# Zero stores of a key and value gradient: one region per group split over 15 and 4 transfer engines, and four regions moved to the end

## The chip, the core and the metric

The kernel runs on one core of a Trainium2 chip. A core has five engines that work on their own instruction queues: PE (TensorE: matrix products and transposes), DVE (VectorE), ACT (ScalarE), POOL (GpSimd) and SP (SyncE, which here only issues transfers). Data between the chip's memory (HBM) and the on-chip memory (SBUF) is moved by sixteen DMA engines, which here are called transfer engines. A transfer (DMA) is issued by SP, ACT or POOL, is cut into packets, and the packets are spread over the transfer engines. Results of matrix products land in PSUM, from which ACT or DVE must copy them ("evacuate" them) to SBUF.

The metric is device time in microseconds (us) of one execution; less is better.

## What is computed

The reference is one decoding step of a transformer block, and the gradient of all its inputs:

```python
xn = layernorm(x)
out = x + attention(xn, k_cache, v_cache, wq, wo) + geglu_ffn(xn, w_gate, w_up, w_down)
out, vjp = jax.vjp(...)
return (out, *vjp(grad_out))
```

Sizes: 4 sequences (b), one new token each, width 512; 32 query heads that share 8 heads (g) of keys and values (four query heads to a head), head width 128; a cache of 4096 positions, of which attention sees only the last 1024; a feed-forward layer of width 1792. All in bf16.

The outputs are the block's output, the gradient of x, and the gradients of the caches and the weights. The gradients of the two caches, dK and dV, have the full shape (4, 8, 4096, 128), although only positions 3072 to 4095 can be different from zero. So each of the 32 pairs (b, g) of dK and of dV has a region of 3072 x 128 bf16 = 768 KB of zeros that must be written. There are 64 such regions, 50.3 MB.

## The kernel before

The feed-forward layer with its gradients comes first. Then the attention part runs over four groups t = 0 to 3 of two key and value heads each (GP = 2), in the loop of lines 766 to 787. For a group:

- masks(t) makes the masked copies of the queries and of the output's gradient (POOL).
- scores(t, 0) transposes the group's keys on TensorE, evacuates the transposed tiles with DVE and multiplies them with the queries; scores(t, 1), also called the dP step, does the same with the values and the output's gradient. The step k = 1 runs the softmax of this group in hooks between its parts (softmax(t), where E_f and P_b are made on ACT and P_x on POOL).
- softmax_d(t) makes the gradient through the softmax. Pieces d1 and d2 put the dV and dK products on a list.
- pre(t + 1) makes queries and the output's gradient of the next group, odq(t) and fin(t) close this one, load_next(t) issues loads for a later group, and dw(t) puts the pieces of the weight products (wo and wq) on the list.

The list is bg. Its pieces are small: one product on TensorE, one evacuation to a staging tile and, with the last piece of a tile, a store. tick(n) (L323) takes up to n of them; it is called between the steps of scores and elsewhere, so that pieces of one group run while the scores of the next are made. Staging tiles are stg_dv and stg_dk (dvdk, around L540; 1 MB per store, 1024 positions of one head for four sequences), osb_o and osb_q (dw, L559 and L571; 512 KB per store). Those stores are issued by SP (helper store, L105), each at its place in SP's order.

The zeros are written by zeros(n) (L303 to L318). It takes the next n regions of dV's and dK's lists, up to four in one transfer, from a zeroed tile ztile in SBUF: 64 of its rows (every second partition) of 12,288 bytes write one region, so that each of the sixteen transfer engines has four rows. These stores are issued by ACT. A manual dependency orders each behind the latest evacuation on ACT, so it takes its place in ACT's order there and waits for nothing of it. The table ZN says how many regions go out in scores(t, k) for head g, after the second of the four tiles:

```python
ZN = ((0, 4, 4, 4), (0, 4, 4, 2), (2, 4, 4, 4), (4, 4, 4, 4))   # index: t, then 2k + g
...
                if q == 1:
                    zeros(ZN[t][GP * k + g])
```

Further regions go out in the feed-forward part, after scores(0, 0), after softmax_d in the last group (zeros(4)), and what remains goes out after the loop (zeros(2 * B * G), where nothing is left here). SP's and ACT's transfers are two hardware queues (q1 and q10 on the page), POOL's a third (q0); q8 brings instructions.

After the loop and the last pieces, the sums over groups are transposed (f_ps), and DVE makes the block's output and the gradient of x, two small stores of four rows (out_b, dx_b).

Of the kernel before, what the change touches and what calls it, by code (L numbers as in the profile page):

```python
# [14 lines left out]
P = 128  # L15
# [3 lines left out]
def kernel(  # L19
# [27 lines left out]
    nc = tc.nc  # L47
# [7 lines left out]
    K0 = Sk - W  # L55
# [5 lines left out]
    GP = 2  # L61
# [26 lines left out]
    last = []  # L88
    chain = []

    def evac(out, in_, n, half=False, eng=None):

        eng = "dve" if half else eng or ("act" if chain else None)
        ca, cd = (190 + n) / 1.2, (120 + (n / 2 if half else n)) / 0.96
        if eng is None:
            eng = "act" if load["act"] + ca <= load["dve"] + cd else "dve"
        load[eng] += ca if eng == "act" else cd
        if eng == "act":
            last.append(nc.scalar.copy(out=out, in_=in_))  # L99
            return last[-1]  # L100
        return nc.vector.tensor_copy(out=out, in_=in_)  # L101

    def store(eng, out, in_, kind, apart):

        d = eng.dma_start(out=out, in_=in_)  # L105
        for k in apart:
            tc.declare_no_dep(d.ins, group=k, reason="stores write disjoint parts of the outputs")
        tc.add_to_no_dep_group(kind, d.ins)
        return d
# [81 lines left out]
    ZP = P // 2  # L191
    ZW = K0 // ZP * Dh
    ztile = const.tile([P, ZW], BF16, name="ztile")
# [83 lines left out]
    def load_w(t):  # L277
        eng = nc.gpsimd if t else nc.sync
        pool = wpool[t % 2]
        wo_t[t] = pool.tile([P, HG, D], BF16, name="wo_sb", tag="wo")  # L280
        eng.dma_start(out=wo_t[t][:], in_=wo_v[t])
        wq_t[t] = pool.tile([P, ND, CW], BF16, name="wq_sb", tag="wq")
        eng.dma_start(out=wq_t[t][:], in_=wq_v[t])

    def load_kv(t, k, g):
        d_, src, nm = ((k_t, A_k_cache, "kb"), (v_t, A_v_cache, "vb"))[k]
        tl = kvpool[(GP * t + g) % (2 * GP)].tile([P, J, Dh], BF16, name=nm, tag=nm)
        (nc.gpsimd if GP * t + g > GP else nc.sync).dma_start(out=tl[:].rearrange("p j d -> p (j d)"),
                          in_=src[:, t * GP + g, K0:Sk, :].rearrange("b (m j) d -> m b (j d)", j=J))
        d_[(t, g)] = tl  # L290
# [9 lines left out]

    zruns = deque([og, 0] for og in (out_2, out_3))

    def zeros(n):  # L303


        zs = ztile[0:P:P // ZP, :]
        while n > 0 and zruns:
            og, r = zruns[0]
            w = min(n, B * G - r, GP * 2)
            zsrc = bass.AP(tensor=zs.tensor, offset=zs.offset, ap=[list(zs.ap[0]), [0, w], [1, ZW]])  # L310
            zdst = og.rearrange("b g s d -> (b g) s d")[r:r + w, 0:K0, :].rearrange("r (m j) d -> m r (j d)", m=ZP)
            z = store(nc.scalar, zdst, zsrc, "zeros", ["rest", "zeros"])
            tc.add_manual_dep(z.ins, last[-1].ins.name,
                              mybir.DependencyInfo(mybir.DependencyClass.NoSync, mybir.DependencyReason.DATA))
            n -= w
            zruns[0][1] += w
            if zruns[0][1] == B * G:
                zruns.popleft()  # L318
# [4 lines left out]
    def tick(n):  # L323
        for _ in range(min(n, len(bg))):
            bg.popleft()()
# [62 lines left out]
                                        in1=msk[:, :, g].unsqueeze(2).broadcast_to([P, NQ, Dh]), op=ALU.mult)  # L388
            st[t][nm] = mr

    ZN = ((0, 4, 4, 4), (0, 4, 4, 2), (2, 4, 4, 4), (4, 4, 4, 4))

    def scores(t, k, hooks):

        lf = (qm, dom)[k]
        blks = (k_t, v_t)[k]
        ps = ps_a.tile([P, WQ], FP32, name="S_ps", tag=("S", "dP")[k])
        for g in range(GP):
            for q in range(NQ):
                T_ps = ps_w.tile([P, JQ, P], BF16, name="T_ps", tag="w")  # L400
                for jj in range(JQ):
                    nc.tensor.transpose(T_ps[:, jj, :], blks[(t, g)][:, q * JQ + jj, :], ident[:])  # L402
                T_sb = tsb.tile([P, WQ, B], BF16, name="T_sb", tag="T", bufs=4)
                evac(T_sb[:].rearrange("p n b -> p (n b)"), T_ps[:].rearrange("p j m -> p (j m)"), 1024, half=True)
                s = q * GP + g
                for b in range(B):
                    nc.tensor.matmul(ps[b * RG:(b + 1) * RG, :], lhsT=lf[:, b, s * RG:(s + 1) * RG],  # L407
                                     rhs=T_sb[:, :, b], start=(g == 0 and q == 0),
                                     stop=(g == GP - 1 and q == NQ - 1), tile_position=(0, b * RG))
                for f in hooks.get(g * NQ + q, ()):  # L410
                    f()
                tick(2 if k or q % 2 else 1)
                if q == 1:
                    zeros(ZN[t][GP * k + g])
        st[t][("S", "dP")[k]] = ps[:]

    def by_batch(src, nm, eng):
# [308 lines left out]
    for f4 in range(NF4):  # L726
        held = {}
        n = min(4, NF - 4 * f4)
# [30 lines left out]
    with tc.tile_pool(name="stage", bufs=4, reuse_waits="tile") as stage, \  # L759
            tc.tile_pool(name="wodd", bufs=1, reuse_waits="tile") as wodd:  # L760
        wpool.append(wodd)
        kvpool.append(wodd)
        load_w(1)
        for k in range(2):
            load_kv(1, k, 1)
        for t in range(NT):
            if t == 0:
                pre(t, {})
            masks(t)
            scores(t, 0, {})  # L770
            zeros(2 if t == 0 else 0)
            scores(t, 1, softmax(t))
            d1, d2 = softmax_d(t)
            zeros(4 if t == NT - 1 else 0)
            if t + 1 < NT:
                pre(t + 1, {0: [d1], 2: [d2]})
            else:
                tick(2)
                d1()
                tick(6)  # L780
                d2()
                tick(2)
            odq(t)
            fin(t)
            load_next(t)
            tick(len(bg))
            dw(t)
        tick(len(bg))
        zeros(2 * B * G)


        acc_r = kvp.tile([P, 2, ND, B, RB], FP32, name="acc_r", tag="kb")
        nc.vector.tensor_copy(out=acc_r[:], in_=acc[:].unsqueeze(4).broadcast_to([P, 2, ND, B, RB]))
        fin_ps = []
        for o in range(2):
            f_ps = ps_w.tile([P, ND, P], FP32, name="f_ps", tag="w")
            for c in range(ND):
                nc.tensor.transpose(f_ps[:, c, :], acc_r[:, o, c].rearrange("p b r -> p (b r)"), ident_f[:])
            fin_ps.append(f_ps[:])
        acc_o, acc_d = fin_ps[0].rearrange("p c d -> p (c d)"), fin_ps[1].rearrange("p c d -> p d c")  # L800

        def adj(x):
            return x[:].rearrange("p (d c) -> p d c", c=ND)

        out_b = kvp.tile([P, D], BF16, name="out_b", tag="vb")
        nc.vector.tensor_tensor(out=out_b[:], in0=acc_o, in1=x_b[:], op=ALU.add)
        nc.sync.dma_start(out=out_0.rearrange("b s d -> (b s) d"), in_=out_b[0:P:RB, :])

        s1 = const.tile([P, 1], FP32, name="s1")
        nc.vector.reduce_sum(out=s1[:], in_=acc_d, axis=AX.XY)  # L810
        pr = kvp.tile([P, D], FP32, name="pr", tag="vb")
        s2 = const.tile([P, 1], FP32, name="s2")
        nc.vector.tensor_tensor_reduce(out=adj(pr), in0=acc_d, in1=adj(xn_f), scale=1.0, scalar=0.0,
                                       op0=ALU.mult, op1=ALU.add, accum_out=s2[:])
        nm1 = const.tile([P, 1], FP32, name="nm1")
        nc.vector.tensor_scalar(out=nm1[:], in0=s1[:], scalar1=-1.0 / D, scalar2=None, op0=ALU.mult)
        nm2 = const.tile([P, 1], FP32, name="nm2")
        nc.vector.tensor_scalar(out=nm2[:], in0=s2[:], scalar1=-1.0 / D, scalar2=None, op0=ALU.mult)
        nc.vector.scalar_tensor_tensor(out=adj(pr), in0=adj(xn_f), scalar=nm2[:, 0:1], in1=acc_d,
                                       op0=ALU.mult, op1=ALU.add)  # L820
        nc.vector.tensor_scalar(out=pr[:], in0=pr[:], scalar1=nm1[:, 0:1], scalar2=rstd[:, 0:1],
                                op0=ALU.add, op1=ALU.mult)
        dx_b = kvp.tile([P, D], BF16, name="dx_b", tag="kb")
        nc.vector.tensor_tensor(out=dx_b[:], in0=pr[:], in1=dy_b[:], op=ALU.add)
        nc.sync.dma_start(out=out_1.rearrange("b s d -> (b s) d"), in_=dx_b[0:P:RB, :])
# [30 lines left out]
```

## Time and profile before

| | us |
|---|---|
| median of 4 runs | 281.8 (281.27 to 282.4) |
| profiled execution, its own time | 281.17 |
| its span in the profile | 279.4 |
| PE busy | 210.5 (75%) |
| DVE busy | 158.4 (57%) |
| ACT busy | 114.8 (41%) |
| POOL busy | 56.0 (20%) |
| time of ACT's transfers (q10: 50.34 MB, 4400 packets) | 42.7% of 16 engines' span |
| time of SP's transfers (q1: 44.58 MB, 12304 packets) | 39.3% |
| time of POOL's transfers (q0: 16.78 MB, 2688 packets) | 15.0% |

All times of the trace count from the start of the span; the profiled execution's own time has 1.8 us more than the span. A row of slices on the page divides the span into 40 equal parts of 7 us, and a digit is the busy share in tenths; the row DMA is the mean over the sixteen transfer engines. ACT issues the zero stores in 0.61 us each: 14 of 3072 KB (from issue to landing 22.3 us in the median) and four of 1536 KB (12.7 us). A transfer lands when the last of its packets has.

The last zero stores are issued at 206.84, 214.12, 220.85, 232.52 and 237.50 us, the first four of them from scores of t = 3, the last behind softmax_d. The last evacuation of a dK piece by ACT ends at 254.8, the first osb_o evacuation of the last weight products on ACT begins at 254.94, and the last osb_q store is issued at 265.95.

### The profile page before, as it was taken

What the parts mean: (1) busy time and instruction counts of PE and PEld (TensorE: products, weight loads), DVE (VectorE), ACT (ScalarE), POOL (GpSimd) and SP (SyncE); (2) the same over time, 40 slices, a digit from 0 to 9 for tenths busy, and PEclk for the clock granted to TensorE, in tenths of its full rate; (3) what the DMA queues carried; (4) which work ended last, traced back from release to release, by engine and by line L of the source; (5) the groups of instructions that cost most, each with busy time, mean ns of one, the idle gap of its engine ahead of it and who ended that gap; (6) DMA issues with size and microseconds to landing.
All of it is one profiled execution on the core that took longest, in us unless ns stands there. A gap on an engine that the chain in (4) does not pass through costs nothing.

```text
span 279.4 us, 7185 instructions
## 1 busy us (share of the span) xinstructions
PE 210.5 (75%) x3126; PEld 137.2 (49%) x3132; DVE 158.4 (57%) x336; ACT 114.8 (41%) x214; POOL 56.0 (20%) x56
## 2 busy tenths in 40 slices
PE   1968976988669879968597978699897765889300
PEld 0856854755445565535365645356664442455200
DVE  6955644555357647654685355477754636276620
ACT  1321642454335236636334445373453442535300
POOL 3890003140200345020006600200520020020000
PEclk9985997799797998999999799999999999597955
DMA  7999999999999999999999999999999999999970
GB/s 239 448 389 429 421 403 396 414 415 425 422 425 426 423 418 417 411 435 421 431 414 354 409 425 426 425 423 427 423 415 427 422 429 422 427 429 425 422 283 20
DMA packets 19423, 112.15 MB, mean 401 GB/s; under 512 B 1456, under 2 KB 5056, under 8 KB 10432
## 3 DMA queue, kind: packets, MB, share of 16 engines
q10 hardware_dynamic: 4400, 50.34, 42.7%
q1 hardware_dynamic: 12304, 44.58, 39.3%
q0 software_dynamic: 2688, 16.78, 15.0%
q8 instruction: 24, 0.39, 0.5%
q14 instruction: 7, 0.06, 0.0%
HBM read 30.68 MB, written 81.01 MB: 400 GB/s over the span
## 4 chain that ended last, share of the span: by engine, by line
PE 45%; DMA 27%; DVE 18%; issue 3%; POOL 1%; ACT 1%; ACTq 0%; DVEq 0%; SPq 0%
DMA out_dram<-osb_q 13%; DMA out_dram<-stg_dk 9%; PE T_ps L402 7%; PE kv_ps L540 6%; DMA out_dram<-osb_g 5%; PE S_ps L407 5%; DVE T_sb L101 4%; PE woT_ps L339 3%; PE wgT_ps L745 3%; DVE woT L101 2%; PE od_ps L512 2%; PE acc_ps L213 2%; PE wqT_ps L598 2%; PE dwg_ps L718 2%; PE dwo_ps L559 2%
## 5 line engine op out<-in xcount | busy, mean ns | idle before, releaser
L101 DVE COPY T_sb<-T_ps 128x1024 bf16<-128x1024 bf16 x64 | 43.8, 690 | 41.0 <-PE T_ps L402 40.5
L99 ACT CAST stg_dv<-kv_ps 128x512 bf16<-128x512 f32 x57 | 30.0, 595 | 31.3 <-PE kv_ps L540 27.9
L99 ACT CAST stg_dk<-kv_ps 128x512 bf16<-128x512 f32 x40 | 22.2, 592 | 37.3 <-PE kv_ps L540 23.8
L540 PE MATMUL kv_ps<-domr,P_x 128*128 128x512 bf16 x63 | 21.5, 404 | 9.6 <-POOL P_x L420 4.8
L387 POOL TENSOR_TENSOR domr<-r,msk 128x512 bf16<-128x512 bf16 x8 | 8.2, 1040 | 73.0 <-DVE r L380 73.0
L402 PE MATMUL T_ps<-ident,kb 128*128 128x128 bf16 x256 | 22.7, 228 | 0.0
L402 PEld LDWEIGHTS <-kb 128*128 128x128 bf16 x256 | 17.8, 103 | 8.6 <-issue 5.8
L99 ACT CAST osb_g<-dwg_ps 128x512 bf16<-128x512 f32 (+1 forms) x28 | 14.1, 539 | 19.0 <-PE dwg_ps L718 8.2
L540 PE MATMUL kv_ps<-qmr,dS_x 128*128 128x512 bf16 x60 | 20.8, 430 | 0.5 <-DVE stg_dk L101 0.2
L402 PE MATMUL T_ps<-ident,vb 128*128 128x128 bf16 x256 | 20.8, 223 | 0.1
L99 ACT CAST osb_o<-dwo_ps 128x512 bf16<-128x512 f32 x25 | 14.6, 586 | 14.0 <-PE dwo_ps L559 13.3
L402 PEld LDWEIGHTS <-vb 128*128 128x128 bf16 x256 | 16.1, 100 | 6.9 <-issue 5.0
L420 POOL TENSOR_TENSOR P_x<-P_b,bmsk 128x1024 bf16<-128x1024 bf16 x4 | 7.6, 1893 | 57.3 <-ACT P_b L468 57.3
L407 PE MATMUL S_ps<-T_sb,dom 128*32 128x256 bf16 x128 | 12.7, 387 | 8.3 <-DVE T_sb L101 7.8
L99 ACT CAST osb_q<-dwq_ps 128x512 bf16<-128x512 f32 x25 | 14.1, 589 | 10.6 <-PE dwq_ps L571 6.1
L101 DVE CAST stg_dk<-kv_ps 128x512 bf16<-128x512 f32 x24 | 16.0, 682 | 1.9 <-PE kv_ps L540 1.8
L101 DVE COPY woT<-woT_ps 128x1024 bf16<-128x1024 bf16 x16 | 11.0, 688 | 9.1 <-PE woT_ps L339 9.1
L407 PE MATMUL S_ps<-T_sb,qm 128*32 128x256 bf16 x128 | 13.1, 387 | 4.0 <-DVE T_sb L101 4.0
L101 DVE COPY wqT<-wqT_ps 128x1024 bf16<-128x1024 bf16 x16 | 11.0, 686 | 5.3 <-PE wqT_ps L598 5.2
L101 DVE COPY wgT<-wgT_ps 128x1024 bf16<-128x1024 bf16 x14 | 9.7, 691 | 7.5 <-PE wgT_ps L745 7.5
L407 PEld LDWEIGHTS <-dom 128*32 128x32 bf16 x128 | 5.3, 93 | 17.1 <-issue 15.3
L559 PE MATMUL dwo_ps<-dyz,od_x 128*128 128x512 bf16 x32 | 13.5, 461 | 0.0
(214 smaller groups left out, 399.6 us busy)
## 6 DMA issues: line engine op xcount, KB each, us to landing
out_dram<-ztile ACTq DMA_DIRECT2D x14, 3072.0 KB, 22.3
out_dram<-stg_dv SPq DMA_DIRECT2D x8, 1024.0 KB, 24.8
out_dram<-stg_dk SPq DMA_DIRECT2D x8, 1024.0 KB, 17.7
out_dram<-ztile ACTq DMA_DIRECT2D x4, 1536.0 KB, 12.7
kb<-in_A_k_cache_dram POOLq DMA_DIRECT2D x5, 1024.0 KB, 20.6
vb<-in_A_v_cache_dram POOLq DMA_DIRECT2D x5, 1024.0 KB, 25.9
out_dram<-osb_o SPq DMA_DIRECT2D x8, 512.0 KB, 15.8
out_dram<-osb_q SPq DMA_DIRECT2D x8, 512.0 KB, 28.4
```

The costliest lines, as they stand in the source:

```text
L99: last.append(nc.scalar.copy(out=out, in_=in_))
L101: return nc.vector.tensor_copy(out=out, in_=in_)
L213: nc.tensor.matmul(ps[:, c, :], lhsT=lf(c), rhs=rhs, start=(k == 0), stop=(k == len(terms) - 1))
L339: nc.tensor.transpose(wT_ps[:, i, c, :], wo_sb[:, 2 * h2 + i, c * P:(c + 1) * P], ident[:])
L387: nc.gpsimd.tensor_tensor(out=mr[:, g], in0=st[t]["r4"][:, k, :].unsqueeze(1).broadcast_to([P, NQ, Dh]), in1=msk[:, :, g].unsqueeze(2).bro ...
L402: nc.tensor.transpose(T_ps[:, jj, :], blks[(t, g)][:, q * JQ + jj, :], ident[:])
L407: nc.tensor.matmul(ps[b * RG:(b + 1) * RG, :], lhsT=lf[:, b, s * RG:(s + 1) * RG], rhs=T_sb[:, :, b], start=(g == 0 and q == 0), stop=(g = ...
L420: eng.tensor_tensor(out=dst[:].rearrange("p j (m b) -> p (j m) b", b=B), in0=src[:].unsqueeze(2).broadcast_to([P, WQ, B]), in1=bmsk[:].uns ...
L512: nc.tensor.matmul(od_ps[r0:r0 + rep * B, 0, :], lhsT=pT[:, j % JQ, (j // JQ) * GP + g:P:NS], rhs=blks[(t, g)][:, j, :], start=(j == 0), s ...
L540: nc.tensor.matmul(mps[:].rearrange("p q d -> p (q d)"), lhsT=src[:, jj, :], rhs=mr[:, g].rearrange("p q d -> p (q d)"), start=True, stop= ...
L559: nc.tensor.matmul(mps[:], lhsT=X[:].rearrange("p h d -> p (h d)")[:, g * rep + i:CW:HG], rhs=dyz[:], start=True, stop=True)
L745: nc.tensor.transpose(wT_ps[:, i, c, :], wsb[:, c, fc * P:(fc + 1) * P], ident[:])
```

## The change

In each group, the call of zeros in scores(t, 0) for the second head is made with part=True. Where this takes a full set of four regions, it issues three transfers in place of one: three regions as before (2304 KB), then of the fourth region the first 60 rows (720 KB, four rows on each of fifteen engines), then the last 4 rows (48 KB, one row on each of four engines). ACT thus issues 26 transfers in place of 18, with the same bytes.

The last entry of ZN for t = 3 goes from 4 to 0, so that no zeros go out in the dP step of the last group for its second head. In place of it, after dw(3) has put the last weight products on the list, two pieces are taken, four regions are issued, and then the rest of the list runs. In ACT's order the zeros(4) behind softmax_d stays where it was among the pieces, and now writes the four regions that the removed call wrote; the new call stands behind the first evacuation of osb_o.

The order of instructions on PE, DVE, POOL and SP is the same as before.

```diff
--- before.py
+++ after.py
@@ -300,18 +300,24 @@
 
     zruns = deque([og, 0] for og in (out_2, out_3))
 
-    def zeros(n):
-
-
-        zs = ztile[0:P:P // ZP, :]
+    def zeros(n, part=False):
+
+
         while n > 0 and zruns:
             og, r = zruns[0]
             w = min(n, B * G - r, GP * 2)
-            zsrc = bass.AP(tensor=zs.tensor, offset=zs.offset, ap=[list(zs.ap[0]), [0, w], [1, ZW]])
-            zdst = og.rearrange("b g s d -> (b g) s d")[r:r + w, 0:K0, :].rearrange("r (m j) d -> m r (j d)", m=ZP)
-            z = store(nc.scalar, zdst, zsrc, "zeros", ["rest", "zeros"])
-            tc.add_manual_dep(z.ins, last[-1].ins.name,
-                              mybir.DependencyInfo(mybir.DependencyClass.NoSync, mybir.DependencyReason.DATA))
+            cuts = [(0, w, 0, ZP)] if not part or w < n else [(0, w - 1, 0, ZP), (w - 1, 1, 0, ZP - ZP // 16),
+                                                              (w - 1, 1, ZP - ZP // 16, ZP)]
+            for r1, nr, m0, m1 in cuts:
+                if nr == 0:
+                    continue
+                zs = ztile[(P // ZP) * m0:(P // ZP) * m1:P // ZP, :]
+                zsrc = bass.AP(tensor=zs.tensor, offset=zs.offset, ap=[list(zs.ap[0]), [0, nr], [1, ZW]])
+                zdst = og.rearrange("b g s d -> (b g) s d")[r + r1:r + r1 + nr, 0:K0, :].rearrange(
+                    "r (m j) d -> m r (j d)", m=ZP)[m0:m1]
+                z = store(nc.scalar, zdst, zsrc, "zeros", ["rest", "zeros"])
+                tc.add_manual_dep(z.ins, last[-1].ins.name,
+                                  mybir.DependencyInfo(mybir.DependencyClass.NoSync, mybir.DependencyReason.DATA))
             n -= w
             zruns[0][1] += w
             if zruns[0][1] == B * G:
@@ -388,7 +394,7 @@
                                         in1=msk[:, :, g].unsqueeze(2).broadcast_to([P, NQ, Dh]), op=ALU.mult)
             st[t][nm] = mr
 
-    ZN = ((0, 4, 4, 4), (0, 4, 4, 2), (2, 4, 4, 4), (4, 4, 4, 4))
+    ZN = ((0, 4, 4, 4), (0, 4, 4, 2), (2, 4, 4, 4), (4, 4, 4, 0))
 
     def scores(t, k, hooks):
 
@@ -411,7 +417,7 @@
                     f()
                 tick(2 if k or q % 2 else 1)
                 if q == 1:
-                    zeros(ZN[t][GP * k + g])
+                    zeros(ZN[t][GP * k + g], part=(k, g) == (0, 1))
         st[t][("S", "dP")[k]] = ps[:]
 
     def by_batch(src, nm, eng):
@@ -785,6 +791,8 @@
             load_next(t)
             tick(len(bg))
             dw(t)
+        tick(2)
+        zeros(4)
         tick(len(bg))
         zeros(2 * B * G)
 
```

## Prediction

> **What bounds the kernel now.** I read the page's row of DMA shares first, then the last windows of the timeline, then the chain that ended last, then the two issuing queues between 199 and 240 us. The page:
>
> ```profile
> DMA  7999999999999999999999999999999999999970
> GB/s 239 448 389 429 421 403 396 414 415 425 422 425 426 423 418 417 411 435 421 431 414 354 409 425 426 425 423 427 423 415 427 422 429 422 427 429 425 422 283 20
> ...
> HBM read 30.68 MB, written 81.01 MB: 400 GB/s over the span
> PE 45%; DMA 27%; DVE 18%; issue 3%; POOL 1%; ACT 1%; ACTq 0%; DVEq 0%; SPq 0%
> ```
>
> The transfer engines are full in 38 of 40 slices, at some 425 GB/s. TensorE is busy 75% of the span, so bytes are the first limit, and only the last two slices are not full. The windows there (columns: span, length, busy time of PE, PEld, DVE, ACT, POOL, granted clock, DMA share, GB/s):
>
> ```profile
> 258.00:268.00 10.00, 3.09 (x16) 1.61 (x14) 6.65 (x13) 2.93 (x6) 0.00 (x0) 0.82 1.00 419
> 268.00:270.00 2.00, 0.00 (x0) 0.00 (x0) 0.00 (x0) 0.00 (x0) 0.00 (x0) 0.50 0.75 297
> 270.00:272.00 2.00, 0.00 (x0) 0.00 (x0) 0.00 (x0) 0.00 (x0) 0.00 (x0) 0.50 0.40 157
> 272.00:278.00 6.00, 0.00 (x0) 0.00 (x0) 0.00 (x0) 0.00 (x0) 0.00 (x0) 0.50 0.07 26
> 278.00:279.40 1.40, 0.00 (x0) 0.00 (x0) 0.00 (x0) 0.00 (x0) 0.00 (x0) 0.50 0.00 0
> ```
>
> From 272 to 278 us nothing computes, and the share is 0.07, which is one sixteenth: a single transfer engine is still at work. Chained by size, queue and end, the packet records give the same: the sixteen engines run without a gap from 2 us, fifteen end between 268.6 and 272.4, one at 277.9. The mean is 270.95, so this engine is 7 us behind the mean and 5.5 behind the next. Its packets are a little slower, not more. A store is landed when its last engine is done, so the lag also shows in landings: the osb_q store issued at 225.65 has fifteen sixteenths at 249.96 and the last at 261.48.
>
> The chain passes through such landings:
>
> ```profile
> 199.59 25.99 DMA out_dram<-stg_dk
> ...
> 225.65 35.83 DMA out_dram<-osb_q
> ...
> 261.58 0.59 ACT osb_q L99
> ```
>
> Why a store waits for a landing is read in the queues (ACT's timeline; the release in brackets):
>
> ```profile
> 214.12 0.61 ACTq L105 DMA_DIRECT2D out_dram<-ztile  x1
> ...
> 220.85 0.61 ACTq L105 DMA_DIRECT2D out_dram<-ztile  x1
> ...
> 223.18 0.51 ACT L468 ACTIVATE P_b<-E_f,rr 128x256 bf16<-128x256 f32 x1 [1.48 <-DVE rr L466]
> ...
> 237.50 0.61 ACTq L105 DMA_DIRECT2D out_dram<-ztile  x1
> 238.15 3.03 ACT L99 CAST stg_dv<-kv_ps 128x512 bf16<-128x512 f32 x6 [3.41 <-DMA out_dram<-osb_o]
> ```
>
> The zero store at 237.50 starts 0.03 us after the osb_o store of 208.98 lands (237.47), a tile that has nothing to do with it. In the order of the program it is the eighth SP or ACT transfer after that one. The osb_q store of 225.65 follows the landing of the eighth before it (stg_dk, 225.58) in the same way, the zero store of 232.52 the stg_dk of 205.88 (232.50), the stg_dv store of 242.99 the osb_o of 214.51 (242.93). So a transfer of these two queues starts only when the eighth before it has landed, and one late engine holds both queues.
>
> **The change, part by part.**
>
> *The split.* Once in each of the four groups a store of four regions (3,072 KB, 64 rows of 12,288 B per region, four rows per engine) becomes one of three regions, one of 60 rows and one of 4 rows. Bytes and rows stay. A 12,288-byte packet took 457 ns from one to the next. The engine that has no part in the 60 rows loses 4 rows x 4 groups = 16 x 0.457 = 7.3 us; four others gain one row each per group, 4 x 0.457 = 1.8 us. The four that the existing four-row transfers (out_b, dx_b) use end at 269.7; with 1.8 they end at 271.5. If the late engine is the one left out, it ends at 277.9 - 7.3 = 270.6, and the last is the next in line, 272.4: 5.5 us gained. If it is another, its bytes are as before and it ends at 277.9 or later: 0. It can't gain rows if it isn't among the four, and it isn't: its chain has no packet of the four-row transfers.
>
> *Which engine that is.* No row names an engine. The late chain carries neither the four-row transfers nor any of the 24 packets of instruction loading (which go over eight engines, three each), which leaves four engines of sixteen. A transfer in less than sixteen parts always uses the same four, so parts are given out from one side, and the engine that fifteen parts leave out is at the other side. The chance lies between one in four (any of the four engines) and one; I take a half, a little nearer to the first end.
>
> [...]
>
> *Eight more issues on ACT.* Four times two, 0.61 us each (median 608 ns in the row of ztile) = 4.9 us of ACT's queue, 1.2 per group. ACT is busy 41%, and waits 27.9 us for kv_ps in stg_dv evacuations, so three of the four lie beside idle time; in the last group I count 0 to 1.2 and take 0, as that group's chain waits for transfers.
>
> *Eight more places in the round of eight.* This is the price. In the last group the three stores stand at 214.12, 214.7 and 215.3. The third now waits for the stg_dv store of 189.30 (landed 219.19): ACT stands 3.9 us, with the osb_q evacuations behind it, and TensorE behind these once its PSUM buffers are full. SP's osb_q of 217.38 now waits for the stg_dk of 199.59 (225.58), 8.2 us; behind it is only the next osb_q, which left at 225.65 anyway. ACT's store of 220.85 now waits for the stg_dk of 205.88 (232.50): up to 11.6 us, with P_b (223.18) behind it, for which POOL's P_x and the dv products wait. The store of 237.50 waits for the osb_o of 214.51 instead of 208.98: 5.5 us. Where landings stay, that is bounded by 0 (all hidden) and 3.9 + 11.6 - 3.4 (the wait that goes) = 12 us on the compute path; I take 7, as TensorE is idle 4.1 of the 19 us from 214 to 233 and 3.6 of the 5 after. Where the late engine is relieved, three groups have taken 3 x 4 x 0.457 = 5.5 us off its lag by then: 219.19 becomes 213.7, 232.50 becomes 227.0, and the stalls are 0 and 6.2, less 1.5 that P_b waits anyway: 4.7 us. That fits under the chain's wait for the osb_q landing, which loses the same 5.5 us and, by the next part, more.
>
> *The move.* The store of four regions at 232.52 goes behind the first osb_o evacuations (after 255 us), past two to four stg_dv and all stg_dk evacuations on ACT, and past SP's last three to four stg stores. 3,146 KB at 425 GB/s is 7.4 us of all engines that no longer lie ahead of the last stg_dv, stg_dk and osb stores. The osb_q landing at 261.48 falls by up to that. What it costs is stock: issued less moved bytes stand at 3.6 MB at 255.6 us; without 3.1 MB there is 0.5 MB, 1.2 us of work, when the moved store comes. The engines run dry for between 0 and, if the compute path is 4.7 us late, 3.5 us; I take 0.7, because most of the 4.7 is under the shortened chain.
>
> *Sum.* Profiled execution: span 279.4, of 281.17 us. DMA end 277.9 - 5.5 + 0.7 = 273.1, so 4.8 us less; 0.3 us is left on the path for the later evacuations: 281.17 - 4.5 = 276.7. The profiled run lies 0.6 under the median of the four (281.8), so against that median the forecast is 277.2; I put 277.0. Its own range: 274.8 (all engines end at the mean) to 279.5 (dry 3.5 us).
>
> **Rivals.**
>
> 1. *The round of eight takes the place (slower).* Place: ACT's store of 220.85, behind a landing that the late engine still sets. It decides if the stg_dk of 205.88 lands after 228 us, that is, if the late engine isn't the one left out. Compute is 7 us later: the last osb_q evacuation is at 261.6 + 7 less what the move gives the chain (up to 4), say 265 to 269, its store is issued 4.4 us later (265.95 against 261.58 before), and the late engine, fed later, ends at 279 to 283 instead of 277.9. 281.8 + 1 to + 5: 283.5 in the middle. For: the eighth-before rule in four rows. Against: those landings must stay.
> 2. *Nothing.* The late engine is another, and the added waits lie beside idle time: its bytes set the end, 277.9 as now, 281.8 +- 0.8.
> 3. *Dry.* Relief comes, but the stock at 255 us is gone and the last 3.1 MB run alone after it: 3.5 us of idle engines and 1 to 2 of unequal ends, 279.5 to 281.
>
> **How the numbers follow.** Relief has 0.51. Of it 0.45 is the forecast, and 0.06 the dry case (0.05 faster, 0.01 same). No relief has 0.49: 0.40 for rival 1, as three waits of 4 to 12 us lie on a queue that feeds TensorE, and 0.09 for nothing. A measurement tells 0.3% (0.85 us) from no change. Faster 0.50, same 0.10, slower 0.40. The range for 8 in 10 must hold both: from 274.8 to 285.5, which leaves out the worst third of rival 1.
>
> **What would show it.** Right: in the last windows no stretch of several us at a share of 0.06 to 0.07; the share falls from 1 to 0 within about 4 us; landings of SP's stores after 200 us come some 5 us earlier and the wait of SP for osb_o (8.6 us) shrinks; the ACT store after the 4 rows stands 5 us or less. Wrong: the stretch of one sixteenth is still there, and ACT stands 8 us or more near 221 with P_b after 229. Dry would be a share under 0.9 between 250 and 260. The forecast is wrong above all if the engine that fifteen parts leave out isn't the late one.

## The result, and the profile after

The changed kernel takes 282.57 us (median of 53 runs) beside 281.57 us for the kernel before (77 runs). The ratio is 1.0032, with a 95% interval of 1.0021 to 1.0044: slower by about 0.9 us, where 277.0 us was forecast, 4.8 us under the 281.8 known then. The time lies inside the stated range, but it is slower, not faster. Single executions of the changed kernel scatter from 280.7 to 284.6, with one at 286.3. The one in its profile took 284.63 us (span 282.8), 2.1 us above their median, so its lines show where the time can go, and more of it than usual. Sizes are therefore taken from the experiments below.

The page of the changed kernel, rows of slices and of the chain:

```profile
DMA  7999999999999999999999999999998999999991
GB/s 241 441 396 428 423 398 420 408 421 425 415 429 417 426 381 417 425 424 353 421 418 408 415 425 421 397 405 427 416 375 343 432 403 368 423 423 376 412 415 48
PE 43%; DMA 26%; DVE 18%; issue 4%; ACT 2%; POOL 1%; ACTq 1%; DVEq 0%; SPq 0%
```

Before, nearly every slice from the 24th on moved 415 to 430 GB/s. Now there are slices of 375, 343, 368 and 376: full by their share, or nearly, but moving less. Two things can make such a slice, packets that take longer and engines that stand idle, and both turn out to be there (in this trace the mean 12,288-byte packet takes 478 ns in place of 465, and the share from 212 to 219 us is 0.84). The last windows of the changed kernel:

```profile
274.00:276.00 2.00, 0.00 (x0) 0.00 (x0) 0.00 (x0) 0.00 (x0) 0.00 (x0) 0.50 1.03 405
276.00:278.00 2.00, 0.00 (x0) 0.00 (x0) 0.00 (x0) 0.00 (x0) 0.00 (x0) 0.50 0.18 70
278.00:280.00 2.00, 0.00 (x0) 0.00 (x0) 0.00 (x0) 0.00 (x0) 0.00 (x0) 0.50 0.09 37
280.00:281.00 1.00, 0.00 (x0) 0.00 (x0) 0.00 (x0) 0.00 (x0) 0.00 (x0) 0.50 0.06 25
```

One engine still runs alone at the end, which the prediction named as a sign that it is wrong, but for 2.4 us in place of 5.5: the last part of the last store lands at 281.71, the one before it at 279.29. The other sign, ACT standing 8 us or more near 221 with P_b after 229, came in part. ACT's timeline:

```profile
178.25 0.67 ACTq L105 DMA_DIRECT2D out_dram<-ztile  x1
179.05 0.51 ACT L474 ACTIVATE P_b<-E_f,rr 128x256 bf16<-128x256 f32 x1 [7.33 <-DMA out_dram<-stg_dk]
...
222.97 2.77 ACTq L105 DMA_DIRECT2D out_dram<-ztile  x2
...
231.19 0.67 ACTq L105 DMA_DIRECT2D out_dram<-ztile  x1
231.99 0.51 ACT L474 ACTIVATE P_b<-E_f,rr 128x256 bf16<-128x256 f32 x1 [2.11 <-DVE T_sb L101]
```

P_b of the last group is computed at 231.99 in place of 223.18. But the long wait lies one group earlier than forecast: in the third group ACT is idle for 7.33 us before P_b, since the zero store in front of it starts only at 178.25, when a stg_dk store has landed (178.23). That is the round of eight as in the trace of before: the zero store starts 0.02 us after the landing of the eighth SP or ACT transfer before it (there 0.02 to 0.07 us, in four rows). The last group's first zero store, at 214.78 in place of 206.84, is then already 8 us late. In the last group itself the zero store of 231.19 also follows such a landing (231.17), but ACT is idle for only 2.1 us there. So much of what the transfer engines lose in this execution lies ahead of the last group's split and of the move:

```profile
205.00:212.00 7.00, 6.45 (x112) 4.83 (x111) 4.31 (x9) 3.52 (x7) 1.06 (x1) 0.98 0.92 381
212.00:219.00 7.00, 7.00 (x63) 4.00 (x61) 4.26 (x7) 3.21 (x6) 2.03 (x2) 0.76 0.84 345
```

### The profile page after: what moved, and what is told of

It is laid out like the page before. It is cut to its first block, busy times and chain, and to the rows that moved or that the text cites. A ratio compares the mean times of both kernels' runs of the same rounds, so it can differ in the third digit from the quotient of the medians.

```text
span 282.8 us, 7189 instructions
## 1 busy us (share of the span) xinstructions
PE 208.0 (74%) x3126; PEld 135.1 (48%) x3132; DVE 158.5 (56%) x336; ACT 114.4 (40%) x214; POOL 56.0 (20%) x56
## 4 chain that ended last, share of the span: by engine, by line
PE 43%; DMA 26%; DVE 18%; issue 4%; ACT 2%; POOL 1%; ACTq 1%; DVEq 0%; SPq 0%
DMA out_dram<-osb_o 11%; PE kv_ps L546 8%; DMA out_dram<-stg_dk 7%; PE T_ps L408 6%; DMA out_dram<-osb_d 5%; PE S_ps L413 4%; DMA out_dram<-ztile 3%; DVE T_sb L101 3%; PE acc_ps L213 3%; PE od_ps L518 3%; PE wqT_ps L604 3%; PE woT_ps L345 2%; PE dwo_ps L565 2%; PE wgT_ps L751 1%; POOL P_x L426 1%
## 5 line engine op out<-in xcount | busy, mean ns | idle before, releaser
L546 PE MATMUL kv_ps<-domr,P_x 128*128 128x512 bf16 x63 | 22.2, 415 | 12.6 <-POOL P_x L426 11.5
L604 PE MATMUL wqT_ps<-ident,wq_sb 128*128 128x128 bf16 x128 | 10.7, 225 | 4.4 <-issue 3.9
```

What stands on the lines that cost most here:

```text
L546: nc.tensor.matmul(mps[:].rearrange("p q d -> p (q d)"), lhsT=src[:, jj, :], rhs=mr[:, g].rearrange("p q d -> p (q d)"), start=True, stop= ...
L604: nc.tensor.transpose(wT_ps[:, i, c, :], wq_sb[:, c, h * Dh:(h + 1) * Dh], ident[:])
```

## The experiments

Two theories stood at the start. A: the late transfer engine takes part in the 60 rows, so the split takes nothing off it. B: it is relieved as forecast, and the gain is lost later. All times stand beside runs of the kernel before on the same chip (medians 281.35 to 281.78).

### The parts of the change alone, and which engine is late

e1_split is the split without the move: in the changed kernel,

```diff
-    ZN = ((0, 4, 4, 4), (0, 4, 4, 2), (2, 4, 4, 4), (4, 4, 4, 0))
+    ZN = ((0, 4, 4, 4), (0, 4, 4, 2), (2, 4, 4, 4), (4, 4, 4, 4))
...
-        tick(2)
-        zeros(4)
         tick(len(bg))
```

> Only the split, in all four groups (eight more issues on ACT, zero stores of the last group where they were). Theory A (the late transfer engine takes part in the 60 rows, so the split takes nothing off it, and the eight extra issues only fill the round of eight): 282 to 284 us beside 281.6, the stretch of one sixteenth at the end is still there, and ACT stands 4 us or more behind a landing in the last group. Theory B (the late engine is relieved as I forecast, but stalls and an idle stretch later eat the gain): the lag of the last engine behind the next is under 3 us in the stores after 200 us.

Measured: 282.85 us, ratio 1.0052 (1.0028 to 1.0076). The time is what theory A expects. But neither of its signs came: no engine runs alone for several us at the end, and in the last group ACT waits at most 2.2 us behind a landing. And the sign that I had set for theory B was there: the lag of the last engine in SP's stores after 200 us is 0.2 to 3.6 us, where it had been 5.5 to 11.5. So a smaller lag isn't relief. The last three engines ended at 278.5, 279.3 and 279.5 us: others had become as late as the late one (below).

e2_move is the move without the split:

```diff
-                    zeros(ZN[t][GP * k + g], part=(k, g) == (0, 1))
+                    zeros(ZN[t][GP * k + g])
```

> Only the move of four regions behind the last weight products, no extra issue. Both theories: SP's and ACT's stores of the last group wait less, since 3 MB no longer stand ahead of them. Theory A: the late engine's bytes are the same and it never idles, so 281.6 within 0.8 us. If the stock of issued bytes runs out near 255 us, 282 to 284, with a DMA share under 0.95 between 250 and 262.

Measured: 281.17 us, ratio 0.9997 (0.9978 to 1.0016). The move alone does nothing, and the DMA share stays at 1.00 or more from 240 to 265 us. The shorter waits that I expected didn't come either: after 199 us ACT waits 7.5 us behind landings, where it waited 5.6, and the osb_q landing that the chain passes through is at 262.27, where it was at 261.48.

e3_once gives the engines the same rows in one place, with one extra issue and without the move:

```diff
-            cuts = [(0, w, 0, ZP)] if not part or w < n else [(0, w - 1, 0, ZP), (w - 1, 1, 0, ZP - ZP // 16),
-                                                              (w - 1, 1, ZP - ZP // 16, ZP)]
+            cuts = [(0, w, 0, ZP)] if not part or w < n else [(0, w, 0, ZP - ZP // 16), (0, w, ZP - ZP // 16, ZP)]
...
-                    zeros(ZN[t][GP * k + g], part=(k, g) == (0, 1))
+                    zeros(ZN[t][GP * k + g], part=(t, k, g) == (0, 0, 1))
```

> The same rows leave and join the same engines as in the change (16 rows off the engine that fifteen parts leave out, four more on each of four engines), but in one store of four regions at t = 0, cut into 4 x 60 and 4 x 4 rows: one extra issue in place of eight, early, and no move. Theory A: 281.6 within 0.8, and the end is one engine alone for 5 us as before. Theory B: the relief shows without its price, 275.5 to 278.

Measured: 285.93 us, ratio 1.0141 (1.0104 to 1.0179), a miss for both theories: one extra issue costs more than eight. In the trace's packet records the cause is plain. Of the 651 zero packets of 12,288 bytes that start between 60 and 95 us, while these two stores run, 121 take more than 700 ns and the mean is 569; before, 2 of 785 and a mean of 463. So packets are slow while a 60-row and a 4-row store run. e1_split shows it at its own places: between 180 and 190 us 14 of 165 take more than 700 ns, up to 1.6 us (before 0 of 198). Over the whole kernel the mean of these 4096 packets is 465 ns before, 471 in e1_split and 483 in e3_once.

e4_probe asks the late engine for its number. On SP's queue, where the lag is largest in the kernel before (11.5 us in its osb_q store of 225.65, 2.9 in ACT's zero store of 214.12), one region of the last group is stored in pieces of k rows, one row to an engine. In the landing records of the changed kernel, beside one early step 1.7 to 1.8 us after the issue, the 4-row store of 224.43 has four landings (235.70 to 237.12) and the 60-row store of 222.97 fifteen (234.96 to 242.32). There is no other split and no move. The main lines:

```diff
+            if part and w == n:
+                cuts, m = [(0, w - 1, 0, ZP)], 0
+                for k in (8, 12, 6, 10, 14, 5, 9):
+                    cuts.append((w - 1, 1, m, m + k))
+                    m += k
...
-                z = store(nc.scalar, zdst, zsrc, "zeros", ["rest", "zeros"])
+                z = store(nc.scalar if m1 - m0 == ZP else nc.sync, zdst, zsrc, "zeros", ["rest", "zeros"])
```

> One region of the last zero store before the dK pieces of the last group goes out on SP's queue in seven small stores of 8, 12, 6, 10, 14, 5 and 9 rows, one row per engine. In the landing record of each, as many sixteenths as it has no rows for should report about 2 us after its issue, and the last sixteenth should be some 9 us behind the one before if, and only if, the late engine takes part. Theory A: the lag appears from some number k of engines on, 5 to 15, and that k names the late engine. Theory B: no probe shows the lag, not even the one of 14. Its time is not of interest (seven more places in the round of eight): 283 to 295.

e10_probe56 is the same with `(5, 6, 4, 5, 6, 6, 16, 16)`:

> The probes again, in the order 5, 6, 4, 5, 6, 6, 16, 16 rows, since the one of 5 came too late in e4_probe, when SP's queue had no backlog left. The probes of 6 should show a last sixteenth some 5 us behind, the probe of 4 none. If the first probe of 5 shows it too, the late engine is the fifth; if not, the sixth.

The landing records of the pieces (time of issue, rows, landing of the last engine but one, of the last engine, us):

```
e4_probe     231.98   8 rows   247.69  253.72
             237.14  12 rows   249.06  254.18
             242.48   6 rows   249.53  254.66
             243.22  10 rows   249.98  255.13
             245.69  14 rows   250.44  256.09
             253.27   5 rows   260.59  260.60   (backlog gone)
             254.04   9 rows   262.18  262.23   (backlog gone)
e10_probe56  232.82   5 rows   248.40  253.42
             237.79   6 rows   248.85  253.88
             243.13   4 rows   249.12  249.33
             243.80   5 rows   249.78  254.38
             245.26   6 rows   250.24  254.82
             252.96   6 rows   260.26  260.37   (backlog gone)
```

As long as SP's queue has a backlog, every piece over five or more engines waits 4.6 to 6.0 us for one of them, and the piece over four doesn't (0.21 us). So the late engine is one that pieces of five rows use and the piece of four doesn't; it is called the fifth here, by that order, since no trace numbers the engines. The pieces of 6 to 14 rows wait for an engine by as much, so I take it for the same one in all of them. Then it takes part in the 60 rows, and theory B's relief can't come: the engine that fifteen parts leave out is another one. Theory A holds on this point. The changed kernel's own trace agrees: of its last 60-row store (issued at 222.97) the last of the fifteen parts lands at 242.32, the one before it at 239.11, while the last of the 4 rows is only 0.65 us behind the next. The times of the two (283.88 and 284.76, one run each) say nothing here.

### Slow packets: from where the rows are read

Theory P says that the packets are slow for the partitions they are read from (the reason that the expectation of e5_ports gives for it was a guess of mine, which no run shows), theory W that it is the place in HBM where they are written, theory L that the eight extra issues cost the time. e5_ports is e1_split with other partitions to read from. Each of the fifteen parts also gets every fifteenth row of the region, so this run alone can't part theory P from theory W:

```diff
+                if m1 - m0 == ZP:
+                    zs, nz, zdst = ztile[0:P:P // ZP, :], nr, rows
+                elif m1 - m0 == 4:
+                    zs, nz, zdst = ztile[32:48:4, :], nr, rows
+                else:
+                    zs, nz = ztile[32:92:4, :], 4
+                    zdst = rows[:, 0, :].rearrange("(i e) w -> e i w", e=15)
+                zsrc = bass.AP(tensor=zs.tensor, offset=zs.offset, ap=[list(zs.ap[0]), [0, nz], [1, ZW]])
```

> The split alone as in e1_split (same issues, same bytes, same rows per engine), but the 60 and 4 rows are read from other partitions of the zeroed tile: part e of fifteen (or four) reads partition 32 + 4e four times (or once). Theory P (in e1_split the packets of these stores took about 1 us in place of 460 ns because several engines read through the same side of SBUF at once): no packets of 700 ns and more near the split stores, mean packet of 12288 bytes 465 to 467 ns as before in place of 471, and 281.0 to 282.0 us in place of 282.85. Theory L (the eight extra issues in the round of eight cost the time): still 282.5 to 283.2. Theory W (the packets are slow for where they are written): still slow packets, 471 ns.

Measured: 281.66 us, ratio 1.0001 (0.9984 to 1.0017). Between 180 and 190 us no packet of 180 is over 700 ns, the mean there is 462, and 467.5 over the whole kernel. The whole loss of e1_split is gone, with the same issues and the same number of rows per engine.

e6_once_ports does the same to e3_once. The main lines:

```diff
-            ... [(0, w, 0, ZP - ZP // 16), (0, w, ZP - ZP // 16, ZP)]
+            ... [(0, w, m, min(m + 15, ZP)) for m in range(0, ZP, 15)]
...
-                zs = ztile[(P // ZP) * m0:(P // ZP) * m1:P // ZP, :]
+                zs = ztile[0:P:P // ZP, :] if m1 - m0 == ZP else ztile[32:32 + 4 * (m1 - m0):4, :]
```

> As e3_once (four regions of t = 0 with 60 rows each over fifteen engines and 4 rows over four), but read as in e5_ports, one row per engine at a time: five issues in place of two. Theory P: the mean of the 12288-byte packets falls from 483 to about 466 ns, and the time from 285.9 to 281 to 282.5. Theory W: 285 or more, packets still at 480 or more.

Measured: 282.21 us, ratio 1.0032 (1.0009 to 1.0056), where e3_once had 1.0141. The mean packet falls from 483 to 467 ns. What is left, 0.3%, I did not take apart.

e7_places keeps the eight extra issues of e1_split and drops the 15 and 4. The main lines:

```diff
-            ... [(0, w - 1, 0, ZP), (w - 1, 1, 0, ZP - ZP // 16),
-                                                              (w - 1, 1, ZP - ZP // 16, ZP)]
+            ... [(0, w - 2, 0, ZP), (w - 2, 1, 0, ZP), (w - 1, 1, 0, ZP)]
```

> Eight more issues as in e1_split (each of the four stores of four regions cut in three), but by whole regions: two, one and one, all of 64 rows over sixteen engines. Theory L: 282.3 to 283.3 as e1_split. Theory P: packets as before (465 ns), 281.0 to 282.0.

Measured: 281.49 us, ratio 1.0003 (0.9986 to 1.0019). Theory L falls for the split alone, although the hold-up that I priced is there in full, in the waits of ACT:

```profile
ACT P_b L473 <- DMA out_dram<-stg_dk: 9.1, 1, 9.1
```

P_b starts at 232.71, 9.5 us later than before, and the time is the same.

e8_narrow changes one line of the kernel before, the partitions that all zero stores are read from:

```diff
-        zs = ztile[0:P:P // ZP, :]
+        zs = ztile[0:ZP, :]
```

> The kernel before with one edit: the 64 rows of all zero stores are read from partitions 0 to 63 in place of every second partition of 128. Nothing else moves. Theory P: packets of the zero stores slow down to 700 ns and more in the mean, 300 us or more. Theory W: 460 ns and 281 to 282 us as before.

Measured: 387.7 us in one run. The destinations are the same, so where a row is read from is enough to make its packet slow (866 ns in the mean in place of 465). For e1_split's own packets theory W has no run of its own. The page:

```profile
DMA  8999999999999999999999999999999999999981
...
q10 hardware_dynamic: 4400, 50.34, 57.5%
q1 hardware_dynamic: 12304, 44.58, 29.3%
...
HBM read 30.68 MB, written 81.01 MB: 289 GB/s over the span
```

The share says full in nearly every slice, as before, while 289 GB/s move in place of 400. The same bytes of ACT's queue take 57.5% of a span of 385.9 us, 222 us per engine, in place of 42.7% of 279.4, 119 us; the mean 12,288-byte packet takes 866 ns in place of 465. A share near 1 isn't work at full speed. An estimate from the means, extra ns x 4096 packets over sixteen engines, gives 1.3 us for e1_split, 4.5 for e3_once and 103 for e8_narrow; measured, beside the kernel before on the same chip, are 1.5, 4.6 and 106.

What e5_ports shows of partitions 32 + 4e is that the packets near the split stores take 462 ns with them. Why these are fast, and partitions 0 to 63 in e8_narrow slow, no run here shows, and no other set was tried for the 60 rows.

### What the move adds

e11_after_ports is the changed kernel with the reading of e5_ports. Against e5_ports it has the move:

```diff
-    ZN = ((0, 4, 4, 4), (0, 4, 4, 2), (2, 4, 4, 4), (4, 4, 4, 4))
+    ZN = ((0, 4, 4, 4), (0, 4, 4, 2), (2, 4, 4, 4), (4, 4, 4, 0))
...
             dw(t)
+        tick(2)
+        zeros(4)
         tick(len(bg))
```

> The changed kernel itself (split and move), with one edit: the 60 and 4 rows are read from partitions 32 + 4e as in e5_ports. If the slow packets are the whole of its loss, 281.0 to 282.0 beside 281.6, and the 12288-byte packets back from 478 to 468 ns or less. If the move together with the split has a price of its own, 282.3 or more.

Measured: 282.66 us, ratio 1.0049 (1.0026 to 1.0072). The packets are repaired (mean 468 ns in place of 478) and the time isn't. Split with good reading costs nothing (e5_ports), move costs nothing (e2_move), both together cost 0.5%. The windows of e11_after_ports:

```profile
240.00:250.00 10.00, 7.91 (x64) 4.09 (x63) 6.02 (x11) 6.11 (x12) 0.00 (x0) 0.92 0.68 284
250.00:255.00 5.00, 4.12 (x153) 3.23 (x150) 3.19 (x7) 0.73 (x2) 1.34 (x1) 1.00 0.97 404
255.00:260.00 5.00, 3.96 (x53) 2.54 (x51) 4.35 (x8) 2.25 (x4) 0.55 (x1) 1.00 0.89 368
260.00:265.00 5.00, 4.97 (x62) 2.62 (x59) 3.53 (x8) 2.68 (x5) 0.00 (x0) 0.72 0.44 178
```

and of e7_places, the same stretches:

```profile
240.00:250.00 10.00, 8.01 (x78) 3.56 (x79) 6.37 (x13) 6.88 (x13) 0.00 (x0) 0.96 0.92 385
250.00:255.00 5.00, 4.04 (x146) 3.05 (x135) 3.51 (x8) 0.33 (x1) 1.89 (x1) 1.00 0.99 413
255.00:260.00 5.00, 4.41 (x94) 3.45 (x93) 3.21 (x8) 1.92 (x4) 0.00 (x0) 1.00 1.02 426
260.00:265.00 5.00, 4.86 (x15) 1.91 (x14) 4.50 (x8) 3.49 (x7) 0.00 (x0) 0.66 0.99 413
```

Both are held up alike at ACT. In e7_places four more regions, issued at 241.01, keep the transfer engines fed, 0.92 and 0.99. In e11_after_ports these are the regions that were moved, and the engines idle 3.2 us of the first stretch and 2.8 of the last; the moved store comes at 262.81 and its 7.4 us (by the prediction's 425 GB/s) then lie near the end. Why these 6 idle us cost only 1.4 us of time is seen in the last store: its last part lands 0.01 us after the one before it, where in e7_places it is 4.2 us behind. So the late engine has caught up, after stretches in which the engines idle 6 us in the mean. Two more runs test the theory. e12_last_whole takes the split out of the last group of e11_after_ports, so that nothing is held up there:

```diff
-                    zeros(ZN[t][GP * k + g], part=(k, g) == (0, 1))
+                    zeros(ZN[t][GP * k + g], part=(k, g) == (0, 1) and t < NT - 1)
```

> e11_after_ports with the split in the first three groups only; the last group's store of four regions is whole again, the move stays. Theory S (extra places in the last group hold up ACT and SP, and with the move there is no stock of issued bytes to cover it): ACT's zero store after the dP step's start goes out near 221 us in place of 233, no stretch between 240 and 265 us with a DMA share under 0.9, and 281.0 to 282.0. Theory R (the 15 and 4 rows themselves leave the engines unequal at the end): 282.3 or more.

Measured: 281.77 us, ratio 0.9999 (0.9981 to 1.0017). ACT's store goes out at 223.89, P_b at 226.22, and the share from 240 to 265 is 1.00 or more.

e13_places_move puts the move on e7_places, which has the extra places and no 15 and 4:

```diff
-    ZN = ((0, 4, 4, 4), (0, 4, 4, 2), (2, 4, 4, 4), (4, 4, 4, 4))
+    ZN = ((0, 4, 4, 4), (0, 4, 4, 2), (2, 4, 4, 4), (4, 4, 4, 0))
...
             dw(t)
+        tick(2)
+        zeros(4)
         tick(len(bg))
```

> e7_places (stores of two, one and one whole regions over sixteen engines in each group) with the move. Theory S: as e11_after_ports, 282.2 to 283.2, with the engines idle at 240 to 250 and 260 to 265 us. Theory R: as e7_places, 281.0 to 282.0.

Measured: 282.33 us, ratio 1.0024 (1.0007 to 1.0042). The share from 240 to 250 is still 0.95; the engines idle from 255 on:

```profile
255.00:260.00 5.00, 4.41 (x88) 3.20 (x86) 3.19 (x8) 1.90 (x4) 0.00 (x0) 0.96 0.74 301
260.00:265.00 5.00, 4.10 (x11) 1.46 (x10) 4.21 (x7) 3.27 (x6) 0.00 (x0) 0.70 0.51 213
```

The last store's last part is 1.1 us behind the one before it. The two runs agree with the theory, though by time alone e13_places_move and e7_places aren't clear of each other (their intervals overlap); the windows tell them apart. The extra places of the last group, together with the move, cost 0.2 to 0.5%. In the changed kernel's own profile the long wait lay in the third group, so that it loses its time in this same way is argued from these runs, not read there.

### A version that beats both

With the fifth engine known to be late, it can be relieved. e9_low4 stores the fourth region of each of the four stores as 48 rows over sixteen engines and 16 rows over the first four, read as in e5_ports and without the move. The main lines:

```diff
-            ... (w - 1, 1, 0, ZP - ZP // 16), (w - 1, 1, ZP - ZP // 16, ZP)]
+            ... (w - 1, 1, 0, 48), (w - 1, 1, 48, ZP)]
...
+                else:
+                    ne = 16 if m1 - m0 == 48 else 4
+                    zs, nz = ztile[32:32 + 4 * ne:4, :], (m1 - m0) // ne
+                    zdst = rows[:, 0, :].rearrange("(i e) w -> e i w", e=ne)
```

> Relief for whatever engine is late beyond the first four: as e5_ports, but the fourth region of each of the four stores goes out as 48 rows over sixteen engines (three each) and 16 rows over four (four each). Each of engines 5 to 16 loses 4 x 0.457 = 1.8 us, each of the first four gains 5.5 us. If the late engine's own bytes set the end, its end falls from 277.9 by up to 1.8 us, while the first four go from 269.7 to 275.2: 279.8 to 281. If the end is set by what the late engine is fed and when, no change: 281.2 to 282.2.

Measured: 279.85 us, ratio 0.9947 (0.9929 to 0.9965), with e5_ports (same issues, 1.0001) as its control. Its last windows:

```profile
270.00:272.00 2.00, 0.00 (x0) 0.00 (x0) 0.00 (x0) 0.00 (x0) 0.00 (x0) 0.50 0.52 205
272.00:274.00 2.00, 0.00 (x0) 0.00 (x0) 0.00 (x0) 0.00 (x0) 0.00 (x0) 0.50 0.30 117
274.00:276.00 2.00, 0.00 (x0) 0.00 (x0) 0.00 (x0) 0.00 (x0) 0.00 (x0) 0.50 0.12 44
276.00:278.00 2.00, 0.00 (x0) 0.00 (x0) 0.00 (x0) 0.00 (x0) 0.00 (x0) 0.50 0.02 6
```

The share now falls step by step, where before one engine ran alone for 6 us. The last landing is 276.92, the one before it 275.49, and the four engines that got the rows end between 274.1 and 275.9 (the landings of dx_b). They are 1 to 3 us short of the late one, so there is little left to shift this way.

e14_low4_early makes the same shift in the first two groups only:

```diff
-                    zeros(ZN[t][GP * k + g], part=(k, g) == (0, 1))
+                    zeros(ZN[t][GP * k + g], part=(k, g) == (0, 1) and t < 2)
...
-            ... [(0, w - 1, 0, ZP), (w - 1, 1, 0, 48), (w - 1, 1, 48, ZP)]
+            ... [(0, w - 2, 0, ZP), (w - 2, 1, 0, 48), (w - 2, 1, 48, ZP),
+                 (w - 1, 1, 0, 48), (w - 1, 1, 48, ZP)]
```

> The relief of e9_low4 (279.85) given in the first two groups alone, two regions each as 48 rows over sixteen and 16 rows over four engines: the same rows per engine and the same eight extra issues, but no extra place in the last two groups. If those places cost e9_low4 something in its last group, 278.5 to 279.6; if its stock covers them, 279.5 to 280.3.

Measured: 284.38 us, ratio 1.0087 (1.0057 to 1.0116), a clear miss of both expectations. The late engine is relieved and the transfer engines run dry elsewhere, in the second group:

```profile
150.00:155.00 5.00, 4.39 (x176) 3.48 (x177) 3.38 (x10) 0.88 (x3) 1.53 (x2) 1.00 0.39 160
155.00:160.00 5.00, 4.71 (x63) 3.31 (x61) 3.61 (x7) 3.64 (x7) 3.47 (x4) 1.00 0.58 184
```

That is 5 us of idle engines in ten (e9_low4 has 0.90 and 0.98 there). ACT waits 5.2 and 4.7 us in front of P_b behind landings of osb_g and osb_o. Five issues in a row held up ACT in the first two groups, and loads and stores of the next came late; that this chain is the cause is argued from these waits, and no run undid it.

## Why the prediction was wrong, step by step

**What bounds the kernel** was right: the transfer engines, one of which ends 5.5 us after the next, as e9_low4 shows by taking 1.8 us off it and gaining 1.8 (0.5%). One reading was off without weight: 37 slices are full, not 38, since the first isn't. And 276.7 scaled to the median of 281.8 is 277.3, not 277.2.

**Which engine that is** is the step that failed: "The chance lies between one in four ... and one; I take a half". The late engine is the fifth, fifteen parts include it, and the 5.5 us of the sum are 0. With that the condition of rival 1 held (no relief). It named the landing that holds up ACT, and its place in the last group, as e5_ports, e7_places, e11_after_ports and e13_places_move show them (P_b waits 9.1 to 9.5 us); in the changed kernel's own profile the wait came a group earlier. The trace of before gave four candidates and no way to choose among them; half was too much for one.

**The rows of the split** were priced by their number and by 457 ns each. What the sum left out is that a packet of the same size took up to 1.6 us when the rows were cut into 15 and 4 and read as before (e1_split), and 462 ns in the mean when they were read from other partitions (e5_ports, where each part also writes other rows). This term was not in the list; in the split alone it is 0.5%, some 1.4 us (1.0052 against 1.0001).

**Eight more issues on ACT**, taken as 0: right, by e7_places (1.0003).

**Eight more places in the round of eight**: the mechanism and the waits were right (the third store behind 219, the next behind 232.5; in e11_after_ports ACT's stores go out at 220.04 and 233.02). The price on the compute path was taken as 7 us and turned by rival 1 into 1 to 5 us at the end (the changed kernel is 0.9 us slower). In time it is 0 while issued bytes last (e5_ports 1.0001, e7_places 1.0003), since the transfer engines are the bound and have work (a share of 0.92 to 1.02 from 240 to 265 us in e7_places).

**The move** was costed at 0.7 us of dry engines, with up to 7.4 us off the chain as its gain. Alone it is worth 0 either way (e2_move, 0.9997), and the osb_q landing doesn't fall. Its real effect is the one of rival 3, in a form that I had not joined to rival 1: the stock that it takes away is what covers the hold-up of the last group. Together they cost 0.7 us (e13_places_move) to 1.4 us (e11_after_ports).

Why the two losses don't add up in the changed kernel (282.57 with slow packets, 282.66 without) isn't shown; that slower packets cost less where engines stand idle anyway would be a guess, which no run tested.

## What to carry to other kernels

If one transfer engine ends late, find out which one before shifting bytes: store small pieces over k engines where its queue has a backlog, and see from which k on a piece lands late. When a transfer is cut so that it uses fewer engines, choose the partitions it is read from anew (here 1.0001 in place of 1.0052), and look at packet durations, because a share near 1 hid packets of 866 ns in place of 465 in e8_narrow. A hold-up on an issuing engine was free here while issued bytes were in stock (P_b 9.5 us later in e7_places at a ratio of 1.0003; with the move 1.0024), so don't take away the stock and add hold-ups in the same stage.

## What was not expected of the hardware

- The same zero stores, read from 64 adjacent partitions in place of every second of 128, take 866 ns per 12,288-byte packet in place of 465, and the kernel 387.7 us (one run) in place of 281.7.
- The fifth of sixteen transfer engines is the late one in the traces in which it was sought (e4_probe, e10_probe56), by 4.6 to 6.0 us at 250 us. Why it is late stays open; no run tried its cause.
- A smaller spread of the engines' ends came with a longer time: the last store's last part is 5.5 us behind the one before it in the kernel before, 0.2 in e1_split (282.85 us), 2.0 in e3_once (285.93) and 0.01 in e11_after_ports (282.66).
